# Row maximum subtracted by 64-row products, products ordered by array form, and constant products in waits

## The chip, the cores and the metric

The kernel runs on one core of a Trainium2 chip. The metric is the device time in microseconds (us) of one execution, the median of several runs. The core has a matrix engine (TensorE), three elementwise engines (VectorE, ScalarE, GpSimd) and DMA queues, here driven by SyncE. In the profile they are called PE, DVE, ACT, POOL and SP; PEld is TensorE's loading of weights.

## The reference, cut to what matters

A recurrence with a complex decay for each feature produces `x`; then a mixture of four single-head attention experts works on `x`, of which each token keeps two.

```python
def _attn_ref(q, k, v, a_re, a_im):
    B, H, S, D = q.shape                      # 4, 8, 768, 48
    mag = np.sqrt(a_re * a_re + a_im * a_im)
    scale = np.minimum(mag, 0.999) / (mag + 1e-06)
    a_re_n, a_im_n = (a_re * scale, a_im * scale)
    for t in range(S):
        ar, ai = (a_re_n[:, :, t, :, None], a_im_n[:, :, t, :, None])
        new_re = ar * S_re - ai * S_im
        new_im = ar * S_im + ai * S_re
        kv = np.einsum('bhd,bhe->bhde', k[:, :, t], v[:, :, t])
        S_re, S_im = (new_re + kv, new_im)
        y[:, :, t] = np.einsum('bhd,bhde->bhe', q[:, :, t], S_re)

def _moe_ref(x, w_gate, wq, wk, wv, wo):      # x: 4 x 768 x 384, 4 experts of 64
    logits = x @ w_gate
    topk = np.argpartition(-logits, 2, axis=-1)[..., :2]
    w = softmax of the two selected logits
    for e in range(E):
        q, k, v = x @ wq[e], x @ wk[e], x @ wv[e]
        scores = np.where(causal, -1000000000.0, 0.125 * (q @ k.T))
        scores = scores - scores.max(-1, keepdims=True)
        a = np.exp(scores)
        a /= a.sum(-1, keepdims=True) + 1e-09
        out += (token selected e) * w * (a @ v @ wo[e])
```

## The kernel before, in words

The program writes down its operations first and emits them afterwards. `Work` records every instruction with a number (4,444 of them), and `Work.run` emits them in the order of the table `ORDER`, chained on each engine, so that an engine's instructions run in exactly this order. `ROOMS` says which buffer of its kind each tile gets. All instructions are emitted at one line, L376; loads of ScalarE's function tables stand at L374, put in whenever the next function needs another table. An instruction starts when those ahead of it on its engine are issued and its inputs and buffers are ready.

**The recurrence.** The 768 steps are cut into six chunks of 128, taken in three pairs, so that the recurrence becomes matrix products within a chunk and a state passed from chunk to chunk. Per batch, three groups of 128 features hold the decay (`ab`) and q and k (`qk`). `quotients`, `arcs`, `magnitudes`, `angles`, `sines` and `products` turn the decay into running magnitudes and phases and multiply them onto q and k; they are elementwise work of ScalarE, VectorE and GpSimd. `regroup` moves the result by DMA from `qk` into `fm`, head by head. Then for each of four head groups `g` (two heads each) and each pair of chunks: `head` transposes k (`pk`), lets ScalarE copy it (`kts`), multiplies k with q (`psc`), and VectorE multiplies by the triangle `keep` (`pts`); `state` makes the update of the state (`pu`), which ScalarE scales into `tst`; `tail` adds the part within the chunk (`yu<-pts,vt`) and that of the state (`yu<-fm,tst`), and ScalarE and VectorE split the sum into a high and a low part, `x`. The first batch goes pair by pair, the later ones whole.

**The experts.** `x` and the weights (`whi`, `wlo`) are used as high and low parts. `proj` makes q and k of two experts at a time (`pp` into `qka`), `vproj` v and the logits (`pv`), `gate` the coefficients. `maxpass` makes the scores once with the query on the partitions (`pm`), of which VectorE takes the row maximum with the causal `mask`; `mrow` transposes these maxima, takes the negative and has them moved by DMA into one row per expert (`mrow`). `score` makes the scores again with the key on the partitions (`psS`): for each block of 128 keys and each of two experts three products of 64 rows, and a fourth that subtracts the row maximum, a row of ones times the row of negative maxima:

```python
            nc.tensor.matmul(y, onerow[64 * e:64 * e + 1, :C], neg[64 * e:64 * e + 1, a0:t1], start=False, stop=True)
        else:
            nc.tensor.matmul(y, a[r, kk, ks], a[r, qq, a0:t1], start=k == 0, stop=False)
```

ScalarE takes the exponential (`pe`), GpSimd cuts the diagonal block to its triangle, `av` multiplies by v (`po`), `total` sums (`dn`), `norm` divides and applies the gate's coefficients (`cb`), and `wo` multiplies by the last weights (`pw`) and writes to `out`.

The experts of one batch and the recurrence of the next are mixed in `ORDER`. A product in 32-bit floats appears twice in the trace, as two passes. The form of a product is the number of array rows and columns that it occupies: 128 rows for `pp` and `psc`, 64 for `psS` and `pm`, and one row for the product with `onerow`.

Of the kernel before, what the change touches and what calls it, by code (L numbers as in the profile page):

```python
# [10 lines left out]
F32 = mybir.dt.float32  # L11
# [11 lines left out]
C = 128  # L23
# [21 lines left out]

ORDER = [
# [901 lines left out]
```

## Time and profile before

| what | value |
| --- | --- |
| median of 3 runs | 577.87 us (574.9 to 583.47) |
| profiled execution, its time | 579.06 us |
| its span in the trace | 577.2 us |
| TensorE, products | 476.2 us busy, 83% of the span |
| ScalarE | 352.0 us, 61% |
| VectorE | 333.6 us, 58% |
| GpSimd | 228.0 us, 40% |
| mean granted clock of TensorE | 0.883 |
| loads of ScalarE's tables | 39, 50.0 us |

The time of an execution is the span and a little around it. Busy shares are means over the whole span; what an engine is worth in a stretch is read from the stretch. The granted clock is 1 at 2.4 GHz and 0.5 at 1.2 GHz.

### The profile page before, as it was taken

The numbers are of one execution on the slowest core, as the hardware profiler recorded it, in microseconds if no ns is written. First come the engines' busy times: TensorE is split into PE (matmuls) and PEld (weight loads), VectorE is DVE, ScalarE is ACT, GpSimd is POOL, SyncE is SP. The second block draws the span as 40 slices with busy tenths as digits, with TensorE's granted clock in tenths as the row PEclk, the third lists the DMA queues.
The fourth block names the chain that finished last, engine by engine and source line by source line (L and its number), as shares of the span: only waits on it lengthen the run. The fifth ranks groups of instructions, "written<-read, shape, count | busy, mean of one in ns | idle before, by whom it ended". The sixth has DMA issues, their size and how long they took to land.

```text
span 577.2 us, 9529 instructions
## 1 busy us (share of the span) xinstructions
PE 476.2 (83%) x3476; PEld 355.7 (62%) x3476; DVE 333.6 (58%) x787; ACT 352.0 (61%) x774; POOL 228.0 (40%) x223
## 2 busy tenths in 40 slices
PE   0025848994989599999987998999989999999996
PEld 0014636883866466678764666688857776777555
DVE  4777824684796255474874485567881371465522
ACT  6999517885675357778856673748772444433353
POOL 2637413614132343764224434554133135201671
PEclk9999975598895878999996996899975899999998
DMA  8432473165552500254444303173231401001002
GB/s 292 190 101 73 116 204 107 43 157 132 130 146 82 166 0 2 49 117 153 151 83 138 84 2 123 43 185 109 51 96 29 124 10 33 15 14 42 29 1 82
DMA packets 22941, 53.42 MB, mean 93 GB/s; under 512 B 3344, under 2 KB 9584, under 8 KB 22768
## 3 DMA queue, kind: packets, MB, share of 16 engines
q1 hardware_dynamic: 22896, 52.83, 32.7%
q8 instruction: 27, 0.44, 0.3%
q14 instruction: 18, 0.15, 0.1%
HBM read 26.74 MB, written 4.72 MB: 55 GB/s over the span
## 4 chain that ended last, share of the span: by engine, by line
PE 63%; ACT 13%; DVE 7%; issue 6%; DMA 6%; POOL 3%; SPq 2%; POOLq 0%; ACTq 0%; DVEq 0%
PE psS L376 13%; PE pp L376 8%; PE yu L376 8%; PE psc L376 6%; PE po L376 6%; PE pw L376 5%; ACT ab L376 5%; DMA fm<-qk 4%; PE pv L376 4%; PE pu L376 4%; PE pm L376 3%; ACT qk L376 3%; PE pk L376 2%; PE dn L376 2%; ACT L374 2%
## 5 line engine op out<-in xcount | busy, mean ns | idle before, releaser
L376 PE MATMUL psc<-fm 96*128 96x128 f32 x384 | 61.1, 309 | 40.9 <-DMA fm<-qk 38.6
L376 POOL TENSOR_TENSOR pe<-pe 128x512 f32<-128x512 f32 (+1 forms) x64 | 77.7, 1215 | 28.5 <-PE po L376 19.1
L376 ACT ACTIVATE pe<-psS 128x512 f32<-128x512 f32 (+2 forms) x96 | 48.9, 540 | 57.0 <-PE psS L376 52.6
L376 PEld LDWEIGHTS psc<-fm 96*128 96x128 f32 x384 | 53.1, 214 | 48.3 <-DMA fm<-qk 39.0
L376 ACT ACTIVATE ab<-ab 128x768 f32<-128x768 f32 (+2 forms) x90 | 55.7, 641 | 19.0 <-POOL qk L376 14.6
L376 PE MATMUL yu<-fm,tst 96*48 96x128 f32 x320 | 50.6, 316 | 17.0 <-ACT tst L376 17.0
L376 PE MATMUL psS<-qka 64*128 64x256 f32 (+3 forms) x480 | 63.1, 367 | 1.5 <-DVE qka L376 1.5
L376 ACT ACTIVATE qk<-qk 128x256 f32<-128x256 f32 (+3 forms) x126 | 59.9, 501 | 7.3 <-DVE qk L376 6.3
L376 DVE CUSTOM_DVE_ANT_0 pm<-pm,mask 128x384 f32<-128x384 f32 (+4 forms) x96 | 47.1, 513 | 23.2 <-PE pm L376 23.1
L376 POOL TENSOR_SCALAR_AFFINE_SELECT pe<-pe 128x256 f32<-128x256 f32 x48 | 20.5, 447 | 95.3 <-ACT pe L376 91.7
L376 PE MATMUL pu<-vt,kts 128*96 128x48 f32 x320 | 41.2, 275 | 19.7 <-ACT kts L376 11.1
L376 PE MATMUL po<-pe,v 128*64 128x256 f32 (+3 forms) x320 | 54.6, 450 | 0.5 <-POOL pe L376 0.5
L376 PEld LDWEIGHTS psS<-qka 64*128 64x128 f32 x480 | 41.6, 217 | 19.4 <-issue 8.6
L376 PEld LDWEIGHTS pu<-vt,kts 128*96 128x96 f32 x320 | 36.7, 189 | 27.1 <-ACT kts L376 12.7
L376 POOL TENSOR_TENSOR qk<-qk 128x768 f32<-128x768 f32 (+1 forms) x27 | 37.9, 1415 | 35.7 <-ACT qk L376 35.7
L376 PE MATMUL yu<-pts,vt 128*64 128x128 f32 x384 | 46.4, 318 | 6.5 <-DVE pts L376 4.3
L374 ACT ACT_TABLE_LOAD x39 | 50.0, 1283 | 1.4 <-PEq L937 0.8
L376 DVE TENSOR_TENSOR pts<-psc,keep 128x512 f32<-128x512 f32 x48 | 32.7, 684 | 28.5 <-PE psc L376 21.4
L376 ACT ACTIVATE tst<-sum,fm 96x48 f32<-96x48 f32 x128 | 38.6, 325 | 17.3 <-DVE sum L376 17.3
L376 PE MATMUL pp<-x,whi 128*128 128x512 f32 (+1 forms) x192 | 46.4, 357 | 1.0 <-ACT ab L376 1.0
L376 DVE TENSOR_TENSOR qk<-qk,ab 128x768 f32<-128x768 f32 (+1 forms) x48 | 38.4, 814 | 12.4 <-POOL qk L376 8.6
L376 PEld LDWEIGHTS yu<-fm,tst 96*48 96x48 f32 x320 | 29.1, 140 | 26.1 <-ACT tst L376 18.4
(102 smaller groups left out, 935.8 us busy)
## 6 DMA issues: line engine op xcount, KB each, us to landing
fm<-qk SPq DMA_DIRECT2D x18, 578.2 KB, 7.3
ab<-in_ak_dram SPq DMA_DIRECT2D x9, 768.0 KB
qk<-in_ak_dram SPq DMA_DIRECT2D x9, 768.0 KB, 4.3
vt<-in_vk_dram SPq DMA_DIRECT2D x16, 384.0 KB, 3.0
fm<-qk SPq DMA_DIRECT2D x24, 192.8 KB, 3.2
out_dram<-ob SPq DMA_DIRECT2D x24, 192.0 KB, 1.9
fm<-qk SPq DMA_DIRECT2D x6, 385.5 KB
x<-yt SPq DMA_DIRECT2D x72, 32.0 KB, 2.8
```

What stands on the lines that cost most here:

```text
L374: chain(engine, nc.scalar.preload_act_table_set(need))
L376: chain(engine, getattr(getattr(nc, engine), method)(*map(real, a), **{x: real(y) for x, y in k.items()}))
```

## The change

Three things change.

First, the product that subtracts the row maximum takes 64 rows in place of one. The two tiles with the negative maxima, `neg0` and `neg1`, are made once, hold zeros in all rows (GpSimd writes them at the start, from a new column of zeros), and the DMA of `mrow` writes rows 0 and 64 of them; `onerow` is used with 64 rows. The zeros add nothing.

Second, `ORDER` and `ROOMS` are new tables, with 4,447 operations in place of 4,444.

Third, a table `WARM` names 18 operations; ahead of each, `run` emits a number of products of two constants, `keep` as weights and 512 columns of `mask` as data, into a PSUM tile that nobody reads. They are 244 in all, 172 of them at one place. The lines that were L376 and L374 are L387 and L385 after the change, and the constants are emitted at L380.

```diff
 ORDER = [
-    0, 18, 8, 3, 20, 26, 24, 19, 25, 23, 39, 21, 41, 33, 40, 51, 22, 42, 14, 9, 81, 82, 27, 72, 52, 73, 74, 34, 60, 61, 54, 31, 75, 76, 62, 63,
...
+WARM = {
+    171: ("psu_4", 172), 185: ("psu_4", 1), 193: ("psu_4", 11), 225: ("psu_4", 3), 252: ("psu_4", 1), 266: ("psu_4", 2), 452: ("psu_4", 1), 392:
+    ("psu_4", 1), 616: ("psu_4", 4), 1130: ("psu_4", 4), 644: ("psu_3", 3), 639: ("psu_3", 2), 838: ("psu_0", 23), 906: ("psu_1", 6), 1330:
+    ("psu_1", 2), 1377: ("psa_1", 1), 4413: ("psa_0", 3), 4419: ("psa_0", 4),
+}
...
             engine, method, a, k = self.ops[i]
+            if i in WARM:
+                room, n = WARM[i]
+                x = self.ps.tile([128, 512], F32, name="warm", tag=room, bufs=1)
+                for _ in range(n):
+                    chain("tensor", nc.tensor.matmul(x, *map(real, self.warm), start=True, stop=True))
...
-    col = new([128, 3], F32, "col")
-    ones, halfpi, eps = (col[:, i:i + 1] for i in range(3))
-    for x, c in ((ones, 1.0), (halfpi, math.pi / 2), (eps, 1e-9)):
+    nc.warm = keep, mask[:, :512]
+    col = new([128, 4], F32, "col")
+    ones, halfpi, eps, zero = (col[:, i:i + 1] for i in range(4))
+    for x, c in ((ones, 1.0), (halfpi, math.pi / 2), (eps, 1e-9), (zero, 0.0)):
         nc.vector.memset(x, c)
...
+    negs = [new([128, S], F32R, f"neg{i}") for i in range(2)]
+    for x in negs:
+        nc.gpsimd.tensor_copy(x, zero.to_broadcast([128, S]))
...
-            t = st["neg", pr] = new([128, S], F32R, "mrow", "mrow")
+            t = st["neg", pr] = negs[pr]
...
                         if kk is None:
-                            nc.tensor.matmul(y, onerow[64 * e:64 * e + 1, :C], neg[64 * e:64 * e + 1, a0:t1], start=False, stop=True)
+                            nc.tensor.matmul(y, onerow[r, :], neg[r, a0:t1], start=False, stop=True)
```

What the tables do to the engines is seen at three places. The first is the start of TensorE's work. Before, its first products are those of the first head group:

```order
L376 MATMUL psc<-fm 128x128 x4
L376 MATMUL pk<-ident,fm 128x96 x4
L376 MATMUL pu<-vt,kts 96x48 x4
L376 MATMUL yu<-pts,vt 64x128 x4
L376 MATMUL yu<-fm,tst 48x128 x2
```

After the change the same place on TensorE reads so, where `keep` is the constant's weights (the piece is the end of the first 172 constants):

```order
L380 LDWEIGHTS keep
L380 MATMUL warm<-mask,keep 128x512
L380 LDWEIGHTS keep
L380 MATMUL warm<-mask,keep 128x512
L387 MATMUL psc<-fm 128x128 x4
L387 MATMUL pk<-ident,fm 128x96 x4
L380 LDWEIGHTS keep
L380 MATMUL warm<-mask,keep 128x512
L387 MATMUL yu<-pts,vt 64x128 x4
L387 MATMUL pu<-vt,kts 96x48 x4
```

All 172 constants of the first place have moved in ahead of the first `psc`; nothing else of TensorE stands before them.

The second place is VectorE's order around the writing of `keep`, a comparison on `iota`. Before, it comes after the running products that carry the first angles:

```order
L376 COPY carry_270<-ab 128x1
L376 SCALAR_TENSOR_TENSOR ab<-ab 128x256
L376 SCALAR_TENSOR_TENSOR qk<-qk 128x256
L376 TENSOR_SCALAR keep<-iota 128x128
L376 SCALAR_TENSOR_TENSOR qk<-cmask,qk 128x256
L376 TENSOR_SCALAR ident<-iota 128x128
L376 TENSOR_TENSOR wlo<-wst,whi 128x1542
L376 TENSOR_TENSOR pts<-psc,keep 128x512
```

After the change, in VectorE's order around the same operation (`qk<-qk,ab` multiplies q by a sine that ScalarE has written to `ab`):

```order
L387 SCALAR_TENSOR_TENSOR ab<-col,carry_253,ab 128x256
L387 SCALAR_TENSOR_TENSOR qk<-cmask,qk 128x256
L387 TENSOR_TENSOR qk<-qk,ab 128x256
L387 TENSOR_SCALAR keep<-iota 128x128
L387 COPY carry_268<-ab 128x1
L387 COPY carry_270<-ab 128x1
L387 TENSOR_TENSOR qk<-qk,ab 128x256
L387 SCALAR_TENSOR_TENSOR ab<-col,carry_270,ab 128x256
```

`keep` now stands between VectorE's first and second product with a sine.

The third place is TensorE at the first score blocks. Before, single blocks stand between products of the next batch's recurrence:

```order
L376 MATMUL psS<-qka 128x256 x6
L376 MATMUL psS<-mrow,onerow 128x256 x2
L376 MATMUL psS<-qka 128x128 x6
L376 MATMUL psS<-mrow,onerow 128x128 x2
L376 MATMUL yu<-pts,vt 64x128 x2
L376 MATMUL yu<-fm,tst 48x128
L376 MATMUL pm<-qka 128x128 x2
L376 MATMUL yu<-fm,tst 48x128
```

After the change the first score blocks on TensorE read so (`neg_73` is the tile `neg0`):

```order
L387 MATMUL psS<-qka 128x256 x6
L387 MATMUL psS<-neg_73,onerow 128x256 x2
L387 MATMUL psS<-qka 128x128 x6
L387 MATMUL psS<-neg_73,onerow 128x128 x2
L387 MATMUL psS<-qka 128x256 x6
L387 MATMUL psS<-neg_73,onerow 128x256 x2
L387 MATMUL psS<-qka 128x256 x6
L387 MATMUL psS<-neg_73,onerow 128x256 x2
L387 MATMUL pm<-qka 128x256 x2
```

The blocks and the `pm` product, all of 64 rows now, stand together, and the recurrence's `yu` products have moved out from between them.

## Rows read from the trace of the kernel before

**Rows 1.** The chain of work that ended last, share of the span by engine.

```profile
PE 63%; ACT 13%; DVE 7%; issue 6%; DMA 6%; POOL 3%; SPq 2%; POOLq 0%; ACTq 0%; DVEq 0%
```

**Rows 2.** Stretches: us, busy time PE PEld DVE ACT POOL, clock, DMA share, GB/s.

```profile
80.70:114.90 34.20, 24.41 (x126) 21.22 (x127) 14.57 (x26) 23.04 (x41) 14.27 (x9) 0.50 0.32 92
170.00:565.40 395.40, 369.02 (x2745) 265.44 (x2741) 221.66 (x545) 224.79 (x481) 159.92 (x155) 0.89 0.26 71
...
425.50:452.80 27.30, 27.01 (x136) 18.16 (x136) 8.63 (x27) 10.28 (x19) 9.43 (x12) 0.50 0.35 92
```

**Rows 3.** Timeline of TensorE from 36 us: start, duration, operation, waits.

```profile
38.62 2.51 PE L376 MATMUL psc<-fm 96*128 96x128 f32 x8 [38.62 <-DMA fm<-qk]
...
52.86 0.87 PE L376 MATMUL pk<-ident,fm 96*128 96x96 f32 x4 [0.38 <-DMA fm<-qk]
54.31 1.51 PE L376 MATMUL pu<-vt,kts 128*96 128x48 f32 x8 [0.58 <-ACT kts L376]
55.62 3.75 PE L376 MATMUL psc<-fm 96*128 96x128 f32 x16
...
60.55 0.88 PE L376 MATMUL pk<-ident,fm 96*128 96x96 f32 x8
```

**Rows 4.** Timeline of ScalarE, VectorE and SyncE, 17 to 44 us.

```profile
17.68 2.24 ACT L376 ACTIVATE qk<-qk 128x256 f32<-128x256 f32 x7
...
32.13 1.20 DVE L376 TENSOR_TENSOR qk<-qk,ab 128x256 f32<-128x256 f32 x2 [0.29 <-ACT ab L376]
...
32.41 0.28 ACT L376 ACTIVATE qk<-qk 128x2 f32<-128x2 f32 x2
...
32.90 1.47 ACT L376 ACTIVATE whi<-wst 128x1542 fp32r<-128x1542 f32 x1
...
35.02 1.34 SPq L376 DMA_DIRECT2D fm<-qk  x2
...
41.28 0.21 DVE L376 TENSOR_SCALAR keep<-iota 128x128 bf16<-128x128 f32 x1
...
43.24 0.47 ACT L376 ACTIVATE kts<-pk 128x384 f32<-128x384 f32 x1
```

**Rows 5.** Groups by line and form: count, busy, mean ns, idle before.

```profile
L374 ACT ACT_TABLE_LOAD x39 | 50.0, 1283 | 1.4 <-PEq L937 0.8
...
L376 POOL TENSOR_SCALAR ab<-ab 128x768 f32<-128x768 f32 x18 | 16.0, 887 | 42.0 <-ACT ab L376 22.0 <-DVE ab L376 19.8
...
L376 POOL TENSOR_TENSOR qk<-ab 128x256 f32<-128x256 f32 x1 | 0.6, 613 | 3.4 <-DMA ab<-in_ak_dram 3.4
```

**Rows 6.** Timeline of TensorE from 478 us, in windows that part the pairs.

```profile
478.13 1.16 PE L376 MATMUL psc<-fm 96*128 96x128 f32 x8
...
482.48 0.62 PE L376 MATMUL psS<-qka 64*128 64x256 f32 x6
...
482.71 0.39 PE L376 MATMUL psS<-qka 64*128 64x256 f32 x4
...
482.82 0.28 PE L376 MATMUL psS<-qka 64*128 64x256 f32 x2
483.03 0.38 PE L376 MATMUL psS<-mrow,onerow 1*128 1x256 f32 x2
483.35 0.62 PE L376 MATMUL psS<-qka 64*128 64x256 f32 x6
```

**Rows 7.** Timeline of TensorE at 434.8 us, two score blocks.

```profile
434.86 1.01 PE L376 MATMUL psS<-qka 64*128 64x256 f32 x6
...
436.31 1.01 PE L376 MATMUL psS<-qka 64*128 64x256 f32 x6
```

**Rows 8.** The chain of waits in order of time: start, us, what.

```profile
109.41 4.13 PE pp L376 x9
...
371.34 4.38 PE pp L376 x18
375.72 2.12 PE pw L376 x12
```

413 rows, old and new, of tables (ORDER, ROOMS) are left out of this document.

## The prediction

> **What bounds the kernel now.** I read the page first. By its chain [rows 1] TensorE holds 63% of the time that sets the end, ScalarE 13%; waits and transfers share the rest. Next come the stretches [rows 2]. From 170 us (the first scores) to 565.4 us TensorE is busy 369.0 of 395.4 us, and ScalarE, the next, 224.8: what shortens TensorE's stream there shortens the run. The same row gives a mean granted clock of 0.89, so 22% of these 395 us, some 87 us, ran at the lower level (1.2 GHz). The longest such stretch [rows 2] is busy 27.01 of 27.30 us, so the low clock is paid in full there.
>
> The start is another matter. TensorE's first product stands at 38.62 us and waits for a DMA [rows 3]. Its `psc` products at 55.62 take 3.75 us for 16, 0.23 each; at 478.13 eight take 1.16, 0.145 each [rows 6]. So TensorE works its first 20 us at the low level. Before the first product everything hangs on ScalarE and VectorE [rows 4]: sine, product with q at 32.13 on VectorE, DMA issue at 35.02, `psc` at 38.62, and only then can ScalarE copy `kts` at 43.24.
>
> **What a change of array form costs.** Form means rows by columns of the array that a product uses: 128x128, 64x128, 128x64, and a single row by 128 for the product with the maximum. The starts tell it [rows 6]. Inside one form the next pair of score products starts 0.11 us after the last (482.71 to 482.82); into the one-row pair it is 0.21, out of it 0.32, and the first pair after the change needs 0.23. A block of eight takes 0.87 (482.48 to 483.35), where four pairs of one form would take 0.45. Two changes of form thus cost 0.42, one 0.21. At the low level a block takes 1.45 [rows 7]; four pairs at twice 0.11 take 0.9, so one change costs 0.27.
>
> The Trainium skill ("TensorEngine Tiling", Key Properties) says that changing the tiling mode drains TensorE; and "TensorE: Matmul & The Clock Gate", in its table "Why this matters for your kernels", that a 32-row product takes the time of a 128-row one. By that the 64-row product costs nothing more than the one-row one, and the whole gain lies in the form. The rows agree on the drain; no row here has the maximum taken off with 64 rows. Without the rule the sum takes that product as one of the score products of its width (0.11 a pair [rows 6]), so it comes to the same.
>
> **The change part by part.**
>
> *The maximum by 64 rows, and products of one form together.* The number of products stays. In the order of TensorE's instructions I count 466 changes of form before and 244 after, leaving the constants out; up to the first score product 62 and 60, after it 404 and 184. So 220 go, all in the stretch that TensorE bounds: 78% at 0.21 and 22% at 0.27 make 49 us. Some of that will reappear as waits: TensorE already stands 26 of these 395 us [rows 2], and a shorter stream meets its suppliers earlier. I take 42, with ends of 20 and 49. The zeroed `neg` tiles are two POOL writes of 128x768. Nearest is POOL's 0.89 us for a pass over that size, 1.8 for two; its first product waits 3.4 us for a load [rows 5], which covers them. I take 0; if a write took twice the nearest row, some 0.2 would stick out. The mask row's DMA now lands in a tile that the scores of the batch before have read long ago: 0.
>
> *The constants ahead of the first product (172).* This is the part that decides. They wait for `keep`, and `keep` is no early constant: before, VectorE makes it at 41.28 [rows 4], since only the mask step after `psc` needs it. In the new order it stands right behind VectorE's first product with q and the sine. When is that? Up to that sine ScalarE has two table loads less (2 x 1.28 [rows 5]), 13 more 256-column passes (7 take 2.24, so 4.2 [rows 4]), one of the two copies of the weights to `whi` (1.5) and seven two-column passes (0.14 each, 1.0): 4.1 us later. Product at 36.2, `keep` done and the constants begin at 36.9. One is a 512-column product with its weights. The nearest rows [rows 8] are `pp` of 512 columns, 0.243 each at full clock, 0.459 at the low one, and `pw`, 2.12 for 12 of 384 columns, 0.177, or 0.236 by columns. I take 0.235: 40.4 us. TensorE comes from rest, though; before, `pk` at 52.86 still takes 0.87 for 4, and at 60.55, after dense work from 54.31 on, 0.88 for 8 [rows 3]. So I let the first 6 us, 13 products, cost 0.22 more: 2.9. The burst ends at 80.2. Without it the first `psc` would start at 38.6 + 4.1 = 42.7, since what follows the product (the issue at 35.02, the DMA, in all 6.5 us [rows 3, 4]) is as before. So instead of filling a wait from zero, the burst fills one of 6 us and overruns it by 37.5; against the run of before the start moves from 38.6 to 80.2, **+42 us**. Queued behind it: on TensorE all heads; on ScalarE `kts`, and with it the angles of the later pieces; on VectorE the mask step and all behind it; on SP the transfers of the next heads, which wait for VectorE. Nothing runs ahead, so I let none of the 42 be absorbed. Ends: 29 (all at `pw`'s 0.177) and 77 (all at 0.459).
>
> The rule that speaks to this: the Trainium skill ("TensorE: Matmul & The Clock Gate", Part 3) has products start and end in strict order, only weight loads being pulled ahead. By that `psc` can't pass the burst. If it could, the rival "free burst" below would hold. No trace of before shows two ready products out of order.
>
> *The other 72 constants.* They stand where TensorE waits for a copy, a mask step or a DMA (11 ahead of the second head's DMA, 23 ahead of the second batch's first one). All of them at 0.235 are 17 us; where the wait is real they are free. Cover: waits of the kind that left 9.8 us idle of the 34 from 80.7 [rows 2]. I take 4 lost, ends 0 and 17.
>
> *Clock.* The burst leaves TensorE warm for the heads. 80.7 to 114.9 ran at the low level, busy 24.4 [rows 2]: up to 12 to gain, 8 taken, since the heads also wait for ScalarE; 3 more for the products before 60 [rows 3]. After 170 us some 80 us of work at the low level remain, 70 once their share of form changes is gone; at full clock 35 less. The low stretches are those of score blocks, where the one-row product takes a third of a block's time; denser blocks and the constants should keep some warm. I take half, 15, ends 0 and 35.
>
> *Table loads.* 39 become 27. Two of the 12 are in the 4.1 above, one more falls between there and `kts`; three between `kts` and the first projection, where ScalarE is the chain: 3 us. The other six are hidden by TensorE.
>
> **Sum.** The profiled run took 579.06 us (span 577.2 and 1.9 around it), 0.2% above the median of 577.87. 579.1 + 42 - 42 + 4 - (8 + 3 + 15) - 3 = **554 us**.
>
> **Rivals.**
> *The burst is free*, because TensorE lets `psc` pass or `keep` comes early: 554 - 37.5 = 516. Against it: `keep` behind the product in the order.
> *No clock is won after 170 us, and little before*: the low stretches follow waits (tst, the row maxima, the DMA of the mask row) that stay. 554 + 15 + 8 = 577. For it: at 425.5 to 452.8 [rows 2] TensorE waits for almost nothing and stays at the low level all the same.
> *Slower: the late start isn't earned back.* One mechanism: TensorE's stream shrinks, but its suppliers in the heads and scores (ScalarE's tst and exponentials, which are in order behind elementwise work) don't move, so that of 42 + 26 us only 25 arrive: 579 + 42 - 25 = 596. It decides from less than 32 us saved after the start (579 + 42 - 32 = 589, 2% above the median). For it: ScalarE's 57% of the stretch, and a wait that grows lets the clock fall. Against it: only 26 us of waits now.
> *The change doesn't do what it says*: if the extra 0.1 to 0.2 us came from new weights and not from the form, joined products would keep it, and the result is that of the slower rival. The starts [rows 6] speak against it, since the extra stands at each change, and a pair with new weights of the same form (482.71 to 482.82) has none.
>
> **How the numbers follow.** Forecast 0.53, free burst 0.10, no clock won 0.22, slower 0.15 (with 0.03 of it for the form). A measurement of this kernel, whose three runs lie 1.5% apart, can tell about 2%, 566 to 589. Of the forecast's own range (535 to 572) a tenth lies above 566. Faster: 0.47 + 0.10 = 0.57; within 2%: 0.06 + 0.22 + 0.01 = 0.29; slower: 0.14. The range 525 to 588 leaves out most of the slower case and half of the free burst.
>
> **What would show it.** First `psc` near 80 us, a solid block of `warm` from 36 us on, its spacing first near 0.46 and then near 0.23, ScalarE and VectorE idle from about 42 to 81. Score blocks in a row at 0.45 to 0.5 us. TensorE's busy time, without `warm`, down by 60 us or more; the mean clock after the start above 0.89. I am wrong if `psc` starts near 42, if the burst stays at 0.46 (first `psc` near 116), or if TensorE's idle time after the start grows by more than 20 us.

## The result and the profile after

The changed kernel took 499.55 us (median of 4 runs, 495.68 to 500.82) against 577.36 us before: a ratio of 0.863, 95% interval 0.855 to 0.871. The forecast was 554 us with a range of 525 to 588. The direction was right, the gain more than three times as large. Times here are medians of all executions, while ratios and their intervals are of fast ones alone, since some executions of a kernel take over 1.5% longer than its fastest.

The chain of work that ended last answers to [rows 1]; the second line is its shares by line:

```profile
PE 60%; ACT 11%; DVE 11%; DMA 7%; POOL 4%; issue 3%; SPq 2%; POOLq 0%; DVEq 0%; ACTq 0%
PE psS L387 9%; PE warm L380 9%; PE pp L387 7%; PE po L387 7%; PE yu L387 6%; PE psc L387 6%; ACT qk L387 5%; PE pw L387 4%; PE pu L387 3%; DVE qk L387 3%; PE pv L387 3%; ACT ab L387 3%; PE pm L387 2%; DMA ab<-in_ak_dram 2%; SPq L387 2%
```

The constants (`warm`) alone hold 9% of the path: most of that is real delay (run 1). The start, on VectorE's timeline, answers to [rows 4], and on TensorE's to [rows 3]:

```profile
35.88 0.89 DVE L387 TENSOR_TENSOR qk<-qk,ab 128x256 f32<-128x256 f32 x1
36.68 0.74 DVE L387 TENSOR_SCALAR keep<-iota 128x128 bf16<-128x128 f32 x1
```

```profile
37.49 39.08 PE L380 MATMUL warm<-mask,keep 128*128 128x512 bf16 x172 [37.49 <-DVE carry L387]
76.40 1.06 PE L387 MATMUL psc<-fm 96*128 96x128 f32 x8
```

`keep` comes behind the first product with a sine, the 172 constants start at 37.5 us, and the first `psc` at 76.4 in place of 38.6. This part went as forecast (36.9 and 80.2). `psc` also takes 1.06 us for eight now, where the first eight took 2.51 [rows 3].

What went differently stands in the stretches from the first product to the first score product (the heads, below) and from there to the end, with the columns of [rows 2]. First the kernel before:

```profile
38.60:169.60 131.00, 98.54 (x696) 82.13 (x697) 86.08 (x188) 89.86 (x206) 50.25 (x46) 0.83 0.47 125
169.60:577.20 407.60, 377.66 (x2782) 273.59 (x2781) 223.70 (x549) 229.12 (x491) 160.32 (x155) 0.89 0.27 72
```

Then the changed kernel:

```profile
76.40:183.30 106.90, 97.32 (x776) 73.39 (x774) 86.78 (x185) 83.51 (x192) 49.25 (x40) 0.98 0.55 143
183.30:497.30 314.00, 301.07 (x2773) 243.28 (x2773) 219.47 (x535) 213.29 (x475) 168.38 (x153) 0.99 0.36 95
```

One figure of these rows misleads. In each trace the record of the clock begins with its first rise, and the time before it counts as 1.00. In the kernel before, that is up to 60.2 us:

```profile
38.60:60.20 21.60, 13.34 (x68) 11.05 (x69) 17.65 (x39) 18.17 (x48) 12.12 (x16) 1.00 0.34 92
```

Yet the `psc` products of this stretch start 0.21 us apart, as they do later at a recorded 0.50; at a recorded 1.00 it is 0.11. Counted at 0.50 up to the first rise, the heads of before ran at 0.75 and not 0.83. In the changed kernel the record begins at 41.1 us, inside the burst, so that its 0.98 stands, and the last stretches are not touched.

The start cost 37.8 us, the heads gained 24.1 (131.0 to 106.9), and the rest gained 93.6 (407.6 to 314.0): together the 79.9 us that lie between the spans. In the last stretch three things are to be read. TensorE's idle time fell from 29.9 us (407.60 less 377.66) to 12.9. The clock rose from 0.89 to 0.99; an estimate of what that cost, the missing share of the clock times the length, is 44.8 us before and 3.1 after. And over the whole run ScalarE's busy time fell from 352.0 to 332.2 us, 15.4 of it in loads of tables, of which 39 [rows 5] became

```profile
L385 ACT ACT_TABLE_LOAD x27 | 34.6, 1283 | 1.2 <-PEq L953 0.8
```

The waits of TensorE, by who ended them (total, times, longest, all in us), tell what the idle time was. Before:

```profile
PE yu L376 <- ACT tst L376: 17.0, 5, 6.5
PE pu L376 <- ACT kts L376: 11.1, 6, 9.1
PE pu L376 <- DVE sum L376: 6.2, 1, 6.2
PE yu L376 <- DVE pts L376: 4.3, 6, 1.3
```

And after:

```profile
PE yu L387 <- DVE pts L387: 1.6, 2, 1.4
...
PE pu L387 <- ACT kts L387: 0.7, 3, 0.3
...
PE yu L387 <- DVE sum L387: 0.6, 2, 0.4
...
PE yu L387 <- ACT tst L387: 0.4, 1, 0.4
```

The two waits for ScalarE went from 28.1 to 1.1 us. One of them, on ScalarE's timeline of the kernel before, shows of what they were made: `tst`, for which TensorE stood 5.48 us, comes behind elementwise passes for later pieces and a load of a table. First TensorE, then ScalarE:

```profile
51.82 0.67 PE L376 MATMUL yu<-fm,tst 96*48 96x128 f32 x4 [5.48 <-ACT tst L376]
```

```profile
48.27 1.28 ACT L374 ACT_TABLE_LOAD   x1
49.56 0.82 ACT L376 ACTIVATE qk<-qk 128x256 f32<-128x256 f32 x3
50.29 0.40 ACT L376 ACTIVATE ab<-ab 128x256 f32<-128x256 f32 x1
50.59 0.40 ACT L376 ACTIVATE qk<-qk 128x256 f32<-128x256 f32 x1
50.90 0.28 ACT L376 ACTIVATE tst<-pu,fm 96x48 f32<-96x48 f32 x1
51.08 0.49 ACT L376 ACTIVATE qk<-qk 128x256 f32<-128x256 f32 x2
51.48 0.28 ACT L376 ACTIVATE tst<-pu,fm 96x48 f32<-96x48 f32 x1
```

### The profile page after: what moved, and what is told of

Read it like the earlier page. It is cut to its first block, busy times and chain, and to the rows that moved or that the text cites. A ratio compares the mean times of both kernels' runs of the same rounds, so it can differ in the third digit from the quotient of the medians.

```text
span 497.3 us, 10026 instructions
## 1 busy us (share of the span) xinstructions
PE 437.3 (88%) x3720; PEld 334.0 (67%) x3720; DVE 338.4 (68%) x788; ACT 332.2 (67%) x762; POOL 239.2 (48%) x225
## 4 chain that ended last, share of the span: by engine, by line
PE 60%; ACT 11%; DVE 11%; DMA 7%; POOL 4%; issue 3%; SPq 2%; POOLq 0%; DVEq 0%; ACTq 0%
PE psS L387 9%; PE warm L380 9%; PE pp L387 7%; PE po L387 7%; PE yu L387 6%; PE psc L387 6%; ACT qk L387 5%; PE pw L387 4%; PE pu L387 3%; DVE qk L387 3%; PE pv L387 3%; ACT ab L387 3%; PE pm L387 2%; DMA ab<-in_ak_dram 2%; SPq L387 2%
## 5 line engine op out<-in xcount | busy, mean ns | idle before, releaser
L380 PE MATMUL warm<-mask,keep 128*128 128x512 bf16 x244 | 58.3, 392 | 37.6 <-DVE carry L387 37.5
L387 POOL TENSOR_TENSOR pe<-pe 128x512 f32<-128x512 f32 (+1 forms) x64 | 80.5, 1259 | 20.6 <-PE po L387 17.7
L380 PEld LDWEIGHTS <-keep 128*128 128x128 bf16 x244 | 24.0, 101 | 66.3 <-DVE keep L387 37.5
L387 DVE TENSOR_TENSOR pts<-psc,keep 128x512 f32<-128x512 f32 x48 | 32.7, 682 | 44.7 <-PE psc L387 42.2
L387 ACT ACTIVATE ab<-ab 128x768 f32<-128x768 f32 (+2 forms) x90 | 56.5, 644 | 8.4 <-DVE ab L387 4.7
L387 ACT ACTIVATE qk<-qk 128x768 f32<-128x768 f32 (+3 forms) x126 | 59.7, 500 | 2.6 <-DVE qk L387 2.1
L387 POOL TENSOR_TENSOR qk<-qk,ab 128x256 f32<-128x256 f32 (+1 forms) x24 | 29.4, 1226 | 60.8 <-ACT ab L387 52.1
L387 ACT ACTIVATE pe<-psS 128x512 f32<-128x512 f32 (+2 forms) x96 | 47.3, 542 | 16.9 <-PE psS L387 14.1
L387 PE MATMUL psc<-fm 96*128 96x128 f32 x384 | 54.2, 286 | 2.0 <-ACT kts L387 1.0
L387 POOL TENSOR_TENSOR qk<-qk 128x768 f32<-128x768 f32 (+1 forms) x27 | 36.4, 1354 | 38.2 <-ACT qk L387 37.6
L387 POOL TENSOR_SCALAR_AFFINE_SELECT pe<-pe 128x256 f32<-128x256 f32 x48 | 26.3, 561 | 57.6 <-ACT pe L387 55.9
L387 DVE CUSTOM_DVE_ANT_0 pm<-pm,mask 128x384 f32<-128x384 f32 (+4 forms) x96 | 46.9, 512 | 10.0 <-PE pm L387 9.8
L387 PEld LDWEIGHTS psc<-fm 96*128 96x128 f32 x384 | 47.3, 194 | 7.8 <-ACT kts L387 2.3
L387 ACT ACTIVATE kts<-pk 128x384 f32<-128x384 f32 (+1 forms) x48 | 20.3, 431 | 44.9 <-PE pk L387 44.7
L387 PE MATMUL pp<-x,whi 128*128 128x512 f32 (+1 forms) x192 | 45.2, 353 | 5.4 <-DMA x<-yt 4.0
L387 ACT ACTIVATE tst<-sum,fm 96x48 f32<-96x48 f32 x128 | 38.9, 326 | 16.3 <-DVE sum L387 16.2
L387 PE MATMUL psS<-qka 64*128 64x256 f32 (+3 forms) x480 | 46.9, 303 | 0.1
L387 PE MATMUL po<-pe,v 128*64 128x256 f32 (+3 forms) x320 | 45.4, 397 | 0.0
L387 PEld LDWEIGHTS psS<-qka 64*128 64x128 f32 x480 | 37.2, 185 | 7.0 <-issue 3.0
L387 DVE TENSOR_TENSOR qk<-qk,ab 128x768 f32<-128x768 f32 (+1 forms) x48 | 39.8, 844 | 3.0 <-POOL qk L387 1.7
L387 PE MATMUL yu<-pts,vt 128*64 128x128 f32 x384 | 37.7, 281 | 2.2 <-DVE pts L387 1.6
L387 PEld LDWEIGHTS pp<-x,whi 128*128 128x128 f32 x192 | 31.7, 194 | 11.4 <-DMA x<-yt 4.1
```

The costliest lines, as they stand in the source:

```text
L380: chain("tensor", nc.tensor.matmul(x, *map(real, self.warm), start=True, stop=True))
L387: chain(engine, getattr(getattr(nc, engine), method)(*map(real, a), **{x: real(y) for x, y in k.items()}))
```

## The experiments

Eleven kernels, each in three rounds beside the kernel before on the same chip. Medians of one kernel before differ between chips (574.2 to 582.0 us), so a difference between runs of different groups is uncertain by several us. Groups: runs 1 to 4; 5 to 7; 8 to 10; 11.

| run | what | us | ratio to before (95%) |
| --- | --- | --- | --- |
| 1 | changed kernel without the burst of 172 | 468.04 | 0.811 (0.800 to 0.822) |
| 2 | `keep` first, burst inside the first wait | 469.27 | 0.814 (0.805 to 0.822) |
| 3 | no constants at all | 487.81 | 0.846 (0.839 to 0.854) |
| 4 | one-row product back, constants kept | 521.11 | 0.904 (0.894 to 0.914) |
| 5 | new order and buffers alone | 516.32 | 0.891 (0.884 to 0.899) |
| 6 | kernel before with the 64-row product | 547.94 | 0.946 (0.938 to 0.953) |
| 7 | kernel before with a warm start | 576.97 | 0.993 (0.984 to 1.003) |
| 8 | run 1 with every load of a table doubled | 513.97 | 0.897 (0.888 to 0.905) |
| 9 | half of the burst | 482.58 | 0.843 (0.835 to 0.851) |
| 10 | the burst without the other constants | 522.73 | 0.912 (0.899 to 0.924) |
| 11 | run 5 with 39 loads of tables | 532.96 | 0.930 (0.924 to 0.937) |

**Run 1.** Is the burst a price, or what pays for the rest?

```diff
-    171: ("psu_4", 172), 185: ("psu_4", 1), 193: ("psu_4", 11), 225: ("psu_4", 3), 252: ("psu_4", 1), 266: ("psu_4", 2), 452: ("psu_4", 1), 392:
+    185: ("psu_4", 1), 193: ("psu_4", 11), 225: ("psu_4", 3), 252: ("psu_4", 1), 266: ("psu_4", 2), 452: ("psu_4", 1), 392:
```

> The 172 constants ahead of the first product are left out, the other 72 stay. Theory A (the burst is a pure delay of the start, and the gain of the change lies in the order and the 64-row product): the first psc comes at 42 to 43 us in place of 76.4, the heads then wait more for ScalarE, so that a third of the 34 us is lost again; 470 to 480 us, granted clock from the first score product to the end at 0.97 or above. Theory B (the delay is what lets the other engines run ahead and keeps TensorE dense and its clock high later): 499 us or more, and the mean clock falls towards 0.9.

468.04 us, first `psc` at 42.2 (42.7 had been forecast for a start without the burst). The burst costs about 31.5 us (499.55 less 468.04) of the 34.2 by which it moves the start. Theory A holds, theory B falls.

**Run 2.** The same constants where they were forecast to be free.

```diff
-        order = ORDER or range(len(self.ops))
+        first = [0, 2, 3, 4]
+        order = first + [i for i in ORDER if i not in first]
```

> All constants stay, but keep and mask are written first of all on VectorE, so that the 172 constants run from about 3 us to about 41 us, inside TensorE's first wait. Theory A: first psc at about 43 us with a high clock, 458 to 472 us, 5 to 12 us better than without the burst. Theory B: no better than 495 us, since the other engines get no time to run ahead.

469.27 us: theory A again, but the 5 to 12 us for a warm start over run 1 were not there. TensorE's timeline, and the stretch from the first score product:

```profile
1.79 39.87 PE L381 MATMUL warm<-mask,keep 128*128 128x512 bf16 x172 [1.79 <-DVE mask L388]
41.94 1.16 PE L388 MATMUL psc<-fm 96*128 96x128 f32 x8 [0.28 <-DMA fm<-qk]
```

```profile
152.50:467.60 315.10, 301.19 (x2773) 243.37 (x2773) 221.25 (x537) 214.33 (x476) 167.54 (x153) 0.99 0.35 95
```

The last stretch takes 315.1 us as against 314.0 in the changed kernel: the late start buys it nothing. Runs 1 and 2 are the fastest versions found, 6% below the changed kernel.

**Run 3.** All constants out.

```diff
-            if i in WARM:
+            if False:
```

> All 244 constants are left out. Theory C (the high clock after the start comes from the denser stream of products of one form): within 8 us of the run without the burst, clock from the first score product on at 0.96 or above. Theory D (it comes from the constants in the waits): 20 us or more above the run without the burst, with stretches of 7 us or longer at the low clock again, mean clock about 0.9.

487.81 us, 19.8 above run 1. Neither theory holds everywhere; the stretches part them:

```profile
42.60:168.50 125.90, 110.12 (x711) 92.85 (x712) 89.75 (x183) 84.88 (x193) 48.55 (x42) 0.86 0.47 121
168.50:486.40 317.90, 304.96 (x2766) 246.83 (x2765) 219.22 (x536) 213.89 (x476) 166.71 (x153) 0.97 0.35 94
```

From the first score product on, the clock stands at 0.97 without a single constant (theory C). In the heads the row gives 0.86, but the record begins at 81.0 us only. On both sides of that:

```profile
42.57 2.08 PE L387 MATMUL psc<-fm 96*128 96x128 f32 x8 [42.57 <-DMA fm<-qk]
...
81.83 1.08 PE L387 MATMUL psc<-fm 96*128 96x128 f32 x8
```

With the time up to 81.0 at 0.50 the heads ran at 0.70. They take 125.9 us as against 110.6 in run 2, at 0.95: there the 72 constants hold the clock (theory D), and the new order alone doesn't lift it (0.75 before).

**Run 4.** The order as changed, the product with one row.

```diff
-                            nc.tensor.matmul(y, onerow[r, :], neg[r, a0:t1], start=False, stop=True)
+                            nc.tensor.matmul(y, onerow[64 * e:64 * e + 1, :], neg[64 * e:64 * e + 1, a0:t1], start=False, stop=True)
```

> The product that takes off the maximum is a one-row product again; order and constants as in the changed kernel. The 80 score blocks then have two more changes of form each, 160 in all: at the 0.21 us that rows of before gave, 34 us more, 533 us at the same clock. If the form of this product matters for the clock as well, 545 us or more and a mean clock below 0.95. If neither, within 5 us of 499.

521.11 us, 21.6 more, and a clock of 0.98 in the last stretch: between the expectations. On TensorE's timeline four blocks of 256 columns stand in a row, first here:

```profile
431.25 0.62 PE L387 MATMUL psS<-qka 64*128 64x256 f32 x6
431.80 0.38 PE L387 MATMUL psS<-neg,onerow 1*128 1x256 f32 x2
432.12 0.62 PE L387 MATMUL psS<-qka 64*128 64x256 f32 x6
```

and in the changed kernel:

```profile
413.58 0.53 PE L387 MATMUL psS<-qka 64*128 64x256 f32 x6
413.93 0.29 PE L387 MATMUL psS<-neg,onerow 64*128 64x256 f32 x2
414.05 0.53 PE L387 MATMUL psS<-qka 64*128 64x256 f32 x6
```

A block takes 0.87 us with one row (431.25 to 432.12), as before [rows 6], and 0.47 with 64 (413.58 to 414.05). That is 0.20 us a change, near the 0.21 of before. But the expectation counted too many changes: where a block stands ahead of products of another form, a change is there in any case, and TensorE's order has 380 of them in place of 244, 136 more and not 160. At 0.20 us that is 27 us, where 0.40 for each of 80 blocks would be 32. From the first score product run 4 reads

```profile
183.80:521.00 337.20, 328.73 (x2773) 250.37 (x2773) 221.12 (x537) 215.08 (x476) 165.68 (x153) 0.98 0.33 88
```

so that TensorE is busy 27.7 us more than in the changed kernel and idle 4.4 us less (8.5 in place of 12.9): waits covered the rest.

**Run 5.** Run 3 and run 4 in one: no constants and one row, so that only order and buffers are new.

> The new order and buffers alone: the one-row product is back and all constants are left out. Theory E (the order is the largest part, because it takes away waits of TensorE): 505 to 520 us, at least 58 us below before, with TensorE's waits after its first product at half of what they were. Theory F (order and 64-row product work only together, through the form): within 25 us of before, 555 us or more.

516.32 us, some 63 below the kernel before by the ratio of 0.891: theory E. From the first score product:

```profile
167.30:516.50 349.20, 337.47 (x2766) 257.75 (x2765) 219.37 (x536) 215.40 (x476) 165.28 (x153) 0.94 0.33 85
```

TensorE is idle 11.7 us there in place of 29.9, and its wait of `yu` for `tst` has gone from 17.0 to 0.4 us. Order and buffers alone take these waits away; which of the two does it no run parts. The clock rises too, 0.89 to 0.94. But the new order also has 86 changes of form fewer than before (380 in place of 466; 84 of them after the first score product) and twelve loads of tables fewer, so this run doesn't show the waits by themselves.

**Run 6.** The other half of the question: before's order with the 64-row product.

```diff
-            t = st["neg", pr] = new([128, S], F32R, "mrow", "mrow")
+            nc.named += 1
+            t = st["neg", pr] = negs[pr]
...
-                            nc.tensor.matmul(y, onerow[64 * e:64 * e + 1, :C], neg[64 * e:64 * e + 1, a0:t1], start=False, stop=True)
+                            nc.tensor.matmul(y, onerow[r, :], neg[r, a0:t1], start=False, stop=True)
...
-        order = ORDER or range(len(self.ops))
+        order = [4444, 0, 4445, 4446] + ORDER[1:]
```

(The last three operations are the column of zeros and the two zeroed tiles.)

> The kernel before with the 64-row product alone: zeroed tiles for the negative maxima, order as before. By the 21.6 us that the one-row product cost in the new order: 557 us. By the 0.21 us a change read in the rows of before, 140 to 160 changes less: 545 us, and lower if the clock follows. If the old order's waits swallow it: 570 us or more.

547.94 us, some 31 less than before by the ratio of 0.946, on 124 changes of form fewer by count. From the first score product, and two of the waits:

```profile
174.10:547.50 373.40, 340.39 (x2782) 261.04 (x2781) 222.96 (x549) 228.06 (x491) 161.36 (x155) 0.93 0.29 79
```

```profile
PE yu L376 <- ACT tst L376: 17.7, 5, 7.0
PE pu L376 <- ACT kts L376: 7.1, 5, 5.4
```

Here the waits stay (33.0 us idle) and the clock still rises from 0.89 to 0.93, in one profiled execution each. TensorE's busy time bears it out: it falls by 37.3 us, more than the 26 that 124 changes at 0.21 us make. So the clock was lower with the one-row products and the changes of form that they bring; whether it is the changes or the single row itself, no run parts. That waits do so by themselves is seen in runs 8 and 11, which add loads to ScalarE and leave TensorE's order as it is.

**Run 7.** A warm start alone.

```diff
+    nc.warm = keep, mask[:, :512]
...
+        first = [0, 2, 3, 4]
+        order = first + [i for i in ORDER if i not in first]
...
+            if engine == "tensor" and "tensor" not in last:
+                x = self.ps.tile([128, 512], F32, name="warm", tag="psu_4", bufs=1)
+                for _ in range(160):
+                    chain("tensor", nc.tensor.matmul(x, *map(real, self.warm), start=True, stop=True))
```

> The kernel before with keep and mask written first on VectorE and 160 constants ahead of TensorE's first product, from about 3 us to about 39 us, inside its first wait; order as before otherwise. If a high clock at the start is worth what the prediction took for the heads: 8 to 11 us less, 568 us. If the clock falls again at the first waits: within 4 us of before.

Not told apart from the kernel before, 0.993 (0.984 to 1.003). The clock between the first product and the first score product:

```profile
39.10:173.10 134.00, 106.41 (x695) 89.09 (x695) 85.37 (x187) 89.97 (x206) 49.82 (x46) 0.71 0.46 123
```

Here the record begins inside the constants, at 5.6 us, so 0.71 is to be compared with the 0.75 worked out above for the kernel before. TensorE entered the heads at 1.00, was busy 1.8 of the first 4.0 us, and the clock was 0.50 from 43.1 to 87.5 us.

**Run 8.** What is a load of a table worth? Run 1 with

```diff
                 if need and need != table:
+                    other = {"trig_and_small": "natural_log_exp_and_others"}.get(need, "trig_and_small")
+                    chain(engine, nc.scalar.preload_act_table_set(other))
```

> The run without the burst (468.0 us), with every load of a ScalarE table preceded by a load of another table: 54 loads in place of 27, 34.7 us more work for ScalarE at 1.28 us each. Theory G (what ScalarE has less to do in the new order is a large part of the gain, since the products wait for its copies and scalings): 490 us or more. Theory H (the prediction's: a load costs only where ScalarE is the chain, at the start and before the first projections): the loads before the first projection, six or seven, add 6 to 10 us, the others nothing; 474 to 478 us.

513.97 us, 45.9 more than run 1 for 34.6 us of loads: theory G, and theory H, which was the prediction's, falls. From the first score product:

```profile
170.50:512.40 341.90, 315.29 (x2773) 253.31 (x2773) 220.65 (x534) 232.00 (x489) 164.06 (x153) 0.96 0.33 87
```

Against run 2, TensorE is idle 26.6 us in place of 13.9, busy 315.3 in place of 301.2 with the same products in the same order, and the clock is 0.96 in place of 0.99: ScalarE's delay comes back as waits, and with them the clock falls.

**Run 9.** 86 constants in place of 172 (`171: ("psu_4", 86)`).

> The changed kernel with 86 constants in place of 172 ahead of the first product, 18.6 us less at the spacing of 0.216 us: first psc at 57.8 us. If each us of the burst beyond the wait is lost in full: 481 us. If the first us of a delay are given back by the engines that run ahead, and later ones are not: 484 us less some, 478 to 481 us. Either is on the straight line between 468.0 (no burst) and 499.55 us, 484, within 5 us; a result of 490 or more would mean that the length beyond half costs little.

482.58 us, 1.2 below the middle of run 1 and the changed kernel; the first `psc` stands at 59.3, not 57.8. Beyond the wait the burst costs nearly its full length.

**Run 10.** The burst alone (`if i == 171:` in place of `if i in WARM:`).

> The 172 constants of the burst stay, the other 72 are left out. Theory I (the prediction's: the burst leaves TensorE warm and the heads keep the clock): first psc at 76.4, low clock between there and the first score product below 30 us in place of the 74.7 us without any constants, 502 to 508 us. Theory J (the clock of the heads is held by the constants in their waits alone): the low stretches come back soon after the burst, 515 to 520 us, that is 31 us above the run without constants.

522.73 us, 34.9 above run 3: theory J. The heads, from the first product on:

```profile
77.80:200.60 122.80, 105.42 (x714) 88.38 (x712) 88.27 (x183) 84.04 (x191) 47.51 (x40) 0.75 0.48 124
```

0.75, where the changed kernel has 0.98 and run 3, without any constants, 0.70 by the working above: the burst leaves next to nothing behind, the small groups of constants in the waits hold the clock. The 72 constants are all that run 10 lacks of the changed kernel, and 15.9 of its 22.4 us more (spans of 519.7 and 497.3) lie in the heads.

**Run 11.** Run 5 with loads of another table ahead of every second of the 27 (up to the 23rd), so that there are 39 as before.

```diff
+                    loads = loads + 1
+                    if loads % 2 and loads < 25:
+                        other = {"trig_and_small": "natural_log_exp_and_others"}.get(need, "trig_and_small")
+                        chain(engine, nc.scalar.preload_act_table_set(other))
```

> The new order alone (one-row product, no constants: 516.3 us) with twelve loads of another table added, ahead of every second of the 27 loads up to the 23rd, so that ScalarE has 39 loads as before. Doubling all 27 cost 46 us, 1.7 us a load: by that 536 us, a third of the 63 us that the order alone gains; with the clock falling too, 540. If the loads matter only where ScalarE is the chain, as the prediction had it (3 us for twelve): 522 us or less.

532.96 us: 16.6 more than run 5 by the medians, 22.6 by the ratios to before (0.930 less 0.891, of 577 us). Close to 536, far from 522. From the first score product:

```profile
173.00:534.40 361.40, 346.39 (x2766) 262.99 (x2765) 222.17 (x537) 223.08 (x482) 163.37 (x153) 0.92 0.31 83
```

TensorE is idle 15.0 us in place of 11.7 in run 5, and the clock is 0.92 in place of 0.94. By this the twelve loads are a quarter to a third of what the order gains; the added ones don't stand where those of before stood, so that it is an estimate.

## Why the prediction was wrong, point by point

**What bounds the kernel.** "What shortens TensorE's stream there shortens the run" was half of it. TensorE was busy 93% of that stretch, but ScalarE's delays reached it directly: run 8 lost more than the ScalarE time that it added.

**The price of a change of form** was right, 0.20 to 0.21 us (block of 0.87 to 0.47), and 49 us for all of it was of the right size: run 6 gained some 31 us on 124 changes, run 5 to run 3 28.5 on 136, both with a rise of the clock in them. The Trainium skill ("TensorEngine Tiling (Array Packing)", Key Properties) says that a change of tiling mode drains TensorE; the two blocks of run 4 agree in that each change costs time, 0.20 us. The rival that the extra came from new weights is refuted by run 4: as many loads of weights in the same order, 0.40 us more a block.

**The first step that failed: "Some of that will reappear as waits".** I took 7 of 49 us off for it. It has the wrong sign: in the new order and buffers TensorE's idle time after the first score product fell by 17.0 us, 29.9 to 12.9, and run 5 shows it without the other two parts (11.7). The waits for ScalarE's `tst` and `kts` went from 28.1 us to 1.1. I had counted the new order's changes of form and not asked, at the waits of before, what stands ahead of `tst` and `kts` on ScalarE.

**The second: table loads, 3 us.** I put six of the twelve at nothing ("the other six are hidden by TensorE"). Run 11 measured 16.6 to 22.6 us for twelve, run 8 1.7 us for each added load of 1.28. Where a load stands ahead of a `tst` or `kts` in ScalarE's order, as at 48.27 us above, TensorE's next product waits for it, and the cover I named, TensorE's own work, was not enough.

**The third: the clock, 8 + 3 + 15.** This term was too small by the most. After the first score product the clock was worth 41.7 us by the estimate above (44.8 less 3.1), where I took 15. The rival without a gain of clock had the low stretches follow waits "that stay", and I gave no reason why they should go. They did not stay. Runs 5, 6 and 3 take the causes apart, as clock of the last stretch: 0.89 before, 0.94 with the order, 0.93 with 64 rows, 0.97 with both. So the clock follows the two other gains, and a term for it can't be set on its own. The longest low stretch after the first score product, in which TensorE was busy nearly all the time [rows 2], fits a rule that I had not weighed: the Trainium skill ("TensorE: Matmul & The Clock Gate", "A second HAM failure mode: psum-queue depth-cycling") tells of a kernel whose TensorE idles briefly and often between groups of products, so that the clock swings between its levels. Run 6 agrees in that the clock rises when the one-row products and the short gaps at their changes of form go; that these gaps are the same mechanism no run here shows.

**"The burst leaves TensorE warm for the heads"** failed as a reason: runs 7 and 10 have the burst and a low clock in the heads, 0.71 and 0.75. The gain is there, but it is that of **the other 72 constants**, which I booked as 4 us lost: they gain 19.8 us (run 3 to run 1), most of it in the heads (run 10). Without its 26 us of clock the sum stands at 580 us, above the kernel before; so the right direction hung on a term of which 8 us had a wrong reason, and was in part luck.

**The burst ahead of the first product** was right in mechanism, place and nearly in size: forecast 37.5 us of overrun, 34.2 in the start (76.4 against 42.2 in run 1), 31.5 in the time. "I let none of the 42 be absorbed" was right within a few us.

**The rivals.** The free burst did not happen: `keep` was where it was said to be, and nothing passed the burst. "Slower" decided from less than 32 us saved after the start; 118 were. "No clock is won" is refuted. No rival had the clock, the waits and the loads all going the same way, and so the range ended too high.

By the medians the gain of 77.8 us is made so: new order alone -61.0 (of it some 17 to 23 for the loads, by run 11), 64 rows -28.5, 72 constants -19.8, burst +31.5. These steps cross groups of runs, so each is uncertain by several us. An estimate of the order's changes of form, 86 at 0.21 us, is 18 us. What the waits and the clock share of the rest can be estimated from the last stretch, 407.6 us before and 349.2 in run 5: of the 58.4 us between them 18.2 are idle time; 40.2 are busy time, some 18 of it for the changes of form, and the other 22 agree with the clock, whose cost falls from 44.8 to 21.0 us. The loads' 17 to 23 us are inside these shares and not beside them.

## What to carry to other kernels

Before you price a new order by what it saves on the busiest engine, go to that engine's waits one by one and read, in the orders before and after, what stands ahead of the awaited instruction on its engine; a load of a table there can cost more than its own time (1.7 us for 1.28 here). Where the clock swings, don't give it a term of its own: it follows waits and changes of form, so forecast both cases of it together with them. Here the constants helped in the waits of the heads and not ahead of the first product; check on what their own operands wait, because a burst that starts late is delay at nearly full price (31.5 of 34.2 us). And before you compare clocks, look where the record of the clock begins.

## What the runs showed of the hardware that was not expected

A TensorE that is almost never waiting can run at the low level for long (27.01 of 27.30 us busy at 0.50 [rows 2]), and taking away the one-row products, with their 124 changes of form, raised the clock after the first score product from 0.89 to 0.93 (run 6). A warm start of 36 us of dense products was worth nothing measurable (run 7, 0.993, interval 0.984 to 1.003), and the clock of the heads behind it was 0.71, as against 0.75 without, with the time before the first recorded rise at 0.50. And 34.6 us of added loads on ScalarE, which is busy 71% of run 1's span, cost 45.9 us, 1.3 times their length (run 8).
